# A static planner given a finer picture of its DMA queue, with merged transposes and a mixed load order

One Trainium2 chip, 1 core. The metric is device time of one execution in microseconds, median of several; lower is better.

## What is computed

```python
def _attn_ref(q, k, v, n_sink, window):        # B, H, S, D = 4, 8, 768, 64; 4 sinks, window 128
    scores = (1 / np.sqrt(D)) * np.matmul(q, k.transpose(0, 1, 3, 2))
    keep = is_sink | in_window                 # causal window of 128, and the first 4 keys
    a = softmax(np.where(keep, scores, -1e9))
    return np.matmul(a, v)
def _moe_ref(x, w_in, w_out, beta):            # 3072 tokens, 512 -> 2048 -> 512
    h = x @ w_in
    return (h / (1 + np.exp(-beta * h))) @ w_out
# reference: _moe_ref(attention output as tokens x 512)      [cut]
```

## The kernel before

The work is cut into eight half batches ("hb", 384 tokens) and each into four units (a pair of heads). Python code in the kernel *plans*: a main loop picks the next step for TensorE (T transpose, SC scores, SS sinks, AV values, OT output transpose, H first FFN product, O second), adds its instructions to a graph with estimated durations, and a pass `arrange` then fixes the order on every engine. On the chip nothing is rescheduled: each engine runs its list in order and waits on semaphores. SyncE's list holds every DMA: loads, stores, and DMA transposes (of q and k for half batches 3 to 7, and of the attention output into `xT` for the same; half batches 0 to 2 are transposed on TensorE).

```python
    def place(self, o, at):                      # the planner's clock
        if o.dma:
            self.free[o.eng] = at + o.queue      # queue: 550, or XQ = 1300 for transposes
            self.dma_free = max(self.dma_free, at + 1100) + 1.15 * o.ns
            o.end = self.dma_free + 1000
    ...
    def choose(n):                               # n neighbouring PSUM banks
        runs = [list(range(i, i + n)) for i in range(9 - n) if not held & set(range(i, i + n))]
        return min(((max(G.bank_at(("B", j)) for j in c), c) for c in runs), default=None)
    ...
    def XT(hb, i, c):                            # q: three transposes, k: one
        n, s0 = "qk"[i], 4 * hb % NT
        cs = [c] if i == 0 else list(range(NK))
        ...
    def XO(u):                                   # one transpose for each unit's output
        ...
    LOADS = xl(0) + xl(1) + list(range(16)) + [x for hb in range(2, NSB) for x in xl(hb)]
    OS = [(T_, t, j) for T_ in range(NSB) for t in range(3) for j in range(4)]
    BACKLOG, AHEAD, MARGIN = 6000, 300, 200
```

`list(range(16))` are the sixteen 512 KB weight blocks (eight of w_in, eight of w_out).

The softmax here doesn't subtract the row's maximum and nothing guards it: scores larger than these inputs give would overflow.

Of the kernel before, what the change touches and what calls it, by code (L numbers as in the profile page):

```python
# [21 lines left out]

class Op:
    __slots__ = ("eng", "fn", "deps", "signal", "count", "waits", "sem", "vc", "dma", "seq", "end", "ns", "alts",
                 "group", "tail", "preds", "ready", "left", "succ", "at", "queue")


class Graph:
# [7 lines left out]
    SKIP = 3  # L36
    SLACK = 0
    COLD, WARM = 217, 150

    def __init__(self):  # L40
        self.ops = []
        self.writers = {}
        self.readers = {}
        self.last_x = {}
        self.free = {e: 800.0 for e in self.ENGINES}
        self.dma_free = 0.0
        self.group = 0
        self.filler, self.fill_to = None, 0
# [5 lines left out]
    def add(self, eng, fn, ns=0, r=(), w=(), x=(), dma=None, alts=None, queue=550):  # L54


        o = Op()
        if alts:
            fn, ns = alts[eng]
        o.eng, o.fn, o.dma, o.ns, o.alts = eng, fn, dma, ns, alts or {eng: (fn, ns)}  # L60
        o.queue = queue
        o.signal, o.count, o.waits, o.vc = False, 0, [], None
        o.group = self.group if eng == "pe" else None
        o.seq = len(self.ops)
        deps = []
        for k in r:
            ws = self.writers.get(k)
            assert ws, k
            deps += [(p, True) for p in ws]
        for k in w:  # L70
            deps += [(p, False) for p in self.readers.get(k, ())]
            deps += [(p, False) for p in self.writers.get(k, ())]
        for k in x:
            deps += [(p, False) for p in self.last_x.get(k, ())]
        o.deps = deps
        for k in r:
            self.readers.setdefault(k, []).append(o)
        for k in w:
            self.writers[k] = [o]
            self.readers[k] = []  # L80
        for k in x:
            self.last_x[k] = [o] if eng == "pe" else self.last_x[k] + [o]
        at = self.free[eng]
        for p, _ in deps:
            at = max(at, p.end + (0 if p.eng == eng and not p.dma else self.HOP))
        self.place(o, at)
        self.ops.append(o)
        return o
# [11 lines left out]
    def place(self, o, at):  # L100
        o.at = at
        if o.dma:
            self.free[o.eng] = at + o.queue
            self.dma_free = max(self.dma_free, at + 1100) + 1.15 * o.ns
            o.end = self.dma_free + 1000
        else:
            o.end = self.free[o.eng] = at + o.ns
# [14 lines left out]
    def arrange(self):  # L122
# [22 lines left out]
        self.free = {e: 800.0 for e in self.ENGINES}  # L145
        self.dma_free = 0.0
# [14 lines left out]
        while todo_pe or pool:  # L161
# [14 lines left out]
            for o in pool:  # L176
                opts = []
                for e, (fn, ns) in o.alts.items():
                    t = max(self.free[e], ready(o, e))
                    if o.dma:  # L180
                        t = max(t, self.dma_free - 3000)
                    opts.append((t + ns, t, e))
                _, t, e = min(opts)
                by_eng.setdefault(e, []).append((t, o))
# [161 lines left out]
def _program(nc, G, sb, ps, q, k, v, w_in, w_out, beta, out):  # L346
    NU = 2 * NPAIR
    NSTG, NX, NV, NT, NE, NON, NG, NTT, NOS, NKS, NWS = 2, 2, 3, 8, 4, 4, 3, 3, 3, 4, 6
    XB = 3
    XQ, XNS = 1300, 700  # L350
# [9 lines left out]
    xT = sb("xT", (128, 4, NTOK), BF16)  # L360
# [12 lines left out]
    onorm = sb("onorm", (128, NK, 2, D), BF16, NON)  # L373
# [10 lines left out]
    def add(eng, fn, ns, r=(), w=(), x=(), dma=None, queue=550):  # L384
        return G.add(eng, fn, ns, r, w, x, dma, None, queue)
# [39 lines left out]
    held = {7}  # L425

    def choose(n):

        runs = [list(range(i, i + n)) for i in range(9 - n) if not held & set(range(i, i + n))]
        return min(((max(G.bank_at(("B", j)) for j in c), c) for c in runs), default=None)  # L430
# [66 lines left out]

    def load(hb, n, i):

        b, t0, z = hb // 2, hb % 2 * HALF, hb % NSTG  # L500
        if n == "v":
            src = v[b, :, t0 + i * 128:t0 + (i + 1) * 128, :].rearrange("h p d -> p h d")
            dst, keys, ns = stg[n][z][:, i, :, :], [i], 262144 / 240
        elif hb >= XB:
            src = {"q": q, "k": k}[n][b, :, t0 + i * 128:t0 + (i + 1) * 128, :].rearrange("h p d -> p h d")
            dst, keys, ns = blocks(stg[n][z])[:, i, :, :], [i], 262144 / 240
        else:
            hs = slice(0, H) if i is None else slice(2 * i, 2 * i + 2)
            src = {"q": q, "k": k}[n][b, hs, t0:t0 + HALF, :].rearrange("h (p j) d -> p h (j d)", j=NK)
            dst = stg[n][z][:, hs, :, :].rearrange("p h j d -> p h (j d)")  # L510
            keys, ns = ([i], 196608 / 350) if i is not None else (range(4), 786432 / 350)
        add("sp", lambda e: e.dma_start(dst, src), ns,  # L512
            w=[("stg", n, z, j) for j in keys], dma=f"d{n}{z}{'' if i is None else i}")

    def load_w(j):
# [6 lines left out]
        add("sp", lambda e: e.dma_start(wst[j % NWS], src), 524288 / 370, w=[("wst", j % NWS)], dma=f"dw{j % NWS}")  # L522
# [10 lines left out]
    def cast(hb, n, i):  # L533
# [5 lines left out]
        elif hb == 0:  # L539
# [10 lines left out]
        if hb == 0 and n != "v":  # L550
# [41 lines left out]
    def XT(hb, i, c):  # L592
        n, s0 = "qk"[i], 4 * hb % NT
        cs = [c] if i == 0 else list(range(NK))
# [3 lines left out]
            x16[n][hb % NX][:, cs[0]:cs[0] + len(cs), :, :].rearrange("p c h d -> p (c h d)")), XNS * len(cs),  # L598
            r=[(n + "16", hb % NX, j, c_) for j in range(4) for c_ in cs],
            w=[("qkT", s0 + j, i, c_) for j in range(4) for c_ in cs], dma=f"dx{n}{c}{hb % 2}", queue=XQ)  # L600
# [87 lines left out]
    def AV(u):  # L688
# [5 lines left out]
        for m, ps in enumerate(parts(half)):  # L694
# [20 lines left out]
            onorm[on][:, :, :, :].rearrange("p m h d -> p (m h) d"), av[:, :, 0:D],  # L715
# [4 lines left out]
    def OT(u):  # L720
# [5 lines left out]
        for m in range(NK):  # L726
            add("pe", lambda e, m=m: nc.tensor.transpose(  # L727
                mp[:, m * 128:(m + 1) * 128], onorm[on][:, m, :, :].rearrange("p h d -> p (h d)"), ident[:, :]),
                mm_ns(128), r=[("on", on), "ident"], x=[("B", bs[0])])
        t0 = b * S + half * HALF  # L730
        any_of(copies(xT[:, hp, t0:t0 + HALF], mp[:, 0:HALF], {"dve": 407, "act": 370}),
# [4 lines left out]
    def XO(u):  # L736
        b, half, hp = where(u)
        on = u % NON
        t0 = b * S + half * HALF
        add("sp", lambda e: e.dma_start_transpose(  # L740
            xT[:, hp, t0:t0 + HALF].rearrange("p (m t) -> p m t", t=128),
            onorm[on][:, :, :, :].rearrange("p m h d -> p (m h d)")), XNS * 0.75,
            r=[("on", on)], w=[("xT", hp, 2 * b + half)], dma=f"dy{on}", queue=XQ)
# [3 lines left out]
    def HQ(T_, m):  # L747
# [4 lines left out]
        t0 = T_ * HALF  # L752
        hp = P[:, bs[0], 0:HALF]
        for c in range(4):
            add("pe", lambda e, c=c: e.matmul(  # L755
                hp, w_in16[:, c, m * 128:(m + 1) * 128], xT[:, c, t0:t0 + HALF],
# [9 lines left out]
    o_bank = []  # L766
    os_i = [0]

    def OQ(T_, t, j):
        G.begin()  # L770
        if j == 0:
            o_bank[:] = take(1)
        bk = o_bank[0]
# [5 lines left out]
        if j == 3:  # L779
# [4 lines left out]
            add("sp", lambda e: e.dma_start(out_t[3 * T_ + t], osb[z][:, :]), 262144 / 300, r=[("osb", z)],  # L784
                dma=f"do{z}")
# [5 lines left out]
    def xl(hb):  # L791
        if hb >= XB:
            return [(hb, n, i) for n in "qkv" for i in range(NK)]
        if hb:
            return [(hb, "q", None), (hb, "k", None)] + [(hb, "v", c) for c in range(NK)]
        return [(0, n, i) for i in range(4) for n in "qk"] + [(0, "v", c) for c in range(NK)]

    LOADS = xl(0) + xl(1) + list(range(16)) + [x for hb in range(2, NSB) for x in xl(hb)]
    CASTS = xl(0) + [(hb, n, i) for hb in range(1, NSB) for n in "qkv" for i in range(NK)]
    HS = [(T_, m) for T_ in range(NSB) for m in range(NM)]  # L800
    OS = [(T_, t, j) for T_ in range(NSB) for t in range(3) for j in range(4)]
    n_cast, n_w, n_xt = [0], [0], [4 * XB]
    BACKLOG, AHEAD, MARGIN = 6000, 300, 200

    def head(s):

        i = done[s]
        if s == "T":
            if i >= 4 * XB or i - NT + 4 >= min(done["SC"], done["SS"]):
                return None  # L810
            if n_cast[0] < (2 * i + 2 if i < 4 else 8 + 9 * (i // 4)):
                return None
# [8 lines left out]
        elif s == "AV":  # L821
            if i >= NU or i >= done["OT"] + NON or i >= min(done["SC"], done["SS"]) or n_cast[0] < 11 + 9 * (i // 4):
# [17 lines left out]
        else:  # L840
# [4 lines left out]
            tb = G.bank_at(("B", o_bank[0])) if j else banks_at(1)  # L845
            if j:
                tb = 0
# [11 lines left out]
    def background():  # L859
# [3 lines left out]
        while moved:  # L863
# [17 lines left out]
            if i < len(CASTS):  # L881
                hb, n, c = CASTS[i]
                t = G.at([("in", hb, n, None if n != "v" and 0 < hb < XB else c)])
# [6 lines left out]
            hb, x_ = n_xt[0] // 4, n_xt[0] % 4  # L890
            if XB <= hb < NSB and n_cast[0] > 11 + 9 * (hb - 1) + (x_ if x_ < 3 else 5) and min(done["SC"], done["SS"]) >= 4 * (hb - hb % 2):
                t = G.at([("qk"[x_ // 3] + "16", hb % NX, 0, x_ if x_ < 3 else 2)])
                if t <= now + AHEAD:
                    XT(hb, x_ // 3, x_ % 3)
                    n_xt[0] += 1
                    if n_xt[0] % 4 == 0:
# [5 lines left out]
            if 4 * XB <= done["OT"] < done["AV"]:  # L902
                t = G.at([("onu", done["OT"])])
                if t <= now + AHEAD:
                    XO(done["OT"])
                    done["OT"] += 1
# [8 lines left out]
    for n_, x in enumerate(xl(0)):  # L915
# [4 lines left out]
        if n_ == 5:  # L920
            add("sp", lambda e: e.dma_start(beta_st[:, :], beta.rearrange("(m p) -> m p", p=128)), 20, w=["beta_st"],
                dma="dbeta")
# [37 lines left out]
    while True:  # L960
# [4 lines left out]
        for s in ("OT", "AV", "SC", "SS", "T") + ffn:  # L965
# [3 lines left out]
            if h[0] + (MARGIN if s in ("OT", "AV", "SC", "SS", "T") else 0) <= now:  # L969
                best = (now, s, h[1])  # L970
                break
            if best is None or h[0] + MARGIN < best[0]:
# [48 lines left out]
```

## Time and profile before

| | before |
|---|---|
| time, median of 3 (range) | 236.48 us (236.27 to 237.78) |
| the profiled execution: time, span | 234.82, 232.9 us |
| TensorE paced work / lost / tail | 203.0 / 26.0 / 3.8 us |
| SyncE transposes | 40 |

*Paced work* is the number of matmuls of each kind times their start-to-start distance in a packed stretch; *lost* is the rest up to the last matmul (the prediction shows how both come out).

### The profile page before, as it was taken

What the parts mean: (1) busy time and instruction counts of PE and PEld (TensorE: products, weight loads), DVE (VectorE), ACT (ScalarE), POOL (GpSimd) and SP (SyncE); (2) the same over time, 40 slices, a digit from 0 to 9 for tenths busy, and PEclk for the clock granted to TensorE, in tenths of its full rate; (3) what the DMA queues carried; (4) which work ended last, traced back from release to release, by engine and by line L of the source; (5) the groups of instructions that cost most, each with busy time, mean ns of one, the idle gap of its engine ahead of it and who ended that gap; (6) DMA issues with size and microseconds to landing.
All of it is one profiled execution on the core that took longest, in us unless ns stands there. A gap on an engine that the chain in (4) does not pass through costs nothing.

```text
span 232.9 us, 4577 instructions
## 1 busy us (share of the span) xinstructions
PE 218.9 (94%) x1756; PEld 122.0 (52%) x1756; DVE 136.8 (59%) x291; ACT 152.6 (66%) x276; POOL 72.5 (31%) x163
## 2 busy tenths in 40 slices
PE   7976999899999999998989999999999999999993
PEld 5554555456555555545446555554555555555541
DVE  3795689977764459527739657946553533633310
ACT  3958978578864889439974757776754655645431
POOL 6584943023450337108355104601740000000000
PEclk9999999999999999999999999999999999999999
DMA  6999999999669998694969999977412111011112
GB/s 182 244 335 245 331 363 389 352 235 228 145 155 237 241 272 162 144 176 72 182 133 232 147 227 222 174 170 169 155 34 65 45 45 45 4 45 45 45 48 90
DMA packets 94677, 39.76 MB, mean 171 GB/s; under 512 B 81328, under 2 KB 87488, under 8 KB 94656
## 3 DMA queue, kind: packets, MB, share of 16 engines
q1 hardware_dynamic: 94656, 39.47, 71.4%
q8 instruction: 14, 0.23, 0.4%
q14 instruction: 7, 0.06, 0.1%
HBM read 27.27 MB, written 6.29 MB: 144 GB/s over the span
## 4 chain that ended last, share of the span: by engine, by line
PE 69%; DMA 9%; DVE 8%; ACT 7%; SPq 4%; issue 1%; POOL 0%
PE P L775 34%; PE P L755 26%; DMA v_stage<-in_v_dram 5%; DMA wst<-in_moe_w_in_dram 4%; DVE g L762 3%; ACT E L645 3%; PE P L708 3%; PE P L637 3%; ACT t L760 2%; SPq L740 2%; SPq L512 2%; DVE vaug L453 2%; DVE onorm L714 1%; ACT qkT L448 1%; PE P L698 1%
## 5 line engine op out<-in xcount | busy, mean ns | idle before, releaser
L760 ACT ACTIVATE t<-P,hbeta 128x384 f32<-128x384 f32 x128 | 73.5, 591 | 43.4 <-PE P L755 39.7
L755 PE MATMUL P<-xT,w_in 128*128 128x384 bf16 x512 | 97.3, 326 | 0.9 <-DVE w_in L453 0.6
L775 PE MATMUL P<-w_out,g 128*128 128x512 bf16 x384 | 96.0, 379 | 2.1 <-DVE g L762 1.9
L762 DVE SCALAR_TENSOR_TENSOR g<-t,P 128x384 bf16<-128x384 f32 x128 | 69.2, 548 | 48.4 <-ACT t L760 46.4
L651 POOL TENSOR_SCALAR_AFFINE_SELECT E<-E 128x512 bf16<-128x512 bf16 (+1 forms) x112 | 54.7, 519 | 68.5 <-ACT E L645 67.9
L755 PEld LDWEIGHTS P<-xT,w_in 128*128 128x128 bf16 x512 | 48.0, 98 | 39.3 <-DVE w_in L453 1.4
L775 PEld LDWEIGHTS P<-w_out,g 128*128 128x128 bf16 x384 | 35.9, 98 | 38.3 <-DVE g L762 4.0
L645 ACT ACTIVATE E<-P 128x768 bf16<-128x768 f32 x64 | 45.5, 777 | 5.6 <-PE P L637 5.5
L448 ACT ACTIVATE osb<-P 128x512 f32<-128x512 f32 x19 | 11.4, 598 | 14.6 <-PE P L775 14.6
L708 PE MATMUL P<-vaug,E 128*128 128x65 bf16 x352 | 19.0, 193 | 1.1 <-DVE vaug L453 0.7
L708 PEld LDWEIGHTS P<-vaug,E 128*128 128x128 bf16 x352 | 16.5, 97 | 4.4 <-DVE vaug L453 0.9
L714 DVE TENSOR_TENSOR onorm<-P,rden 128x384 bf16<-128x384 f32 x32 | 17.7, 554 | 0.9 <-DMA xT<-onorm 0.2
L637 PE MATMUL P<-qkT 64*128 64x128 bf16 (+1 forms) x256 | 16.8, 239 | 1.5 <-ACT E L645 1.3
L453 DVE CAST q<-q_stage 128x512 bf16<-128x512 f32 (+1 forms) x19 | 10.1, 541 | 8.5 <-DMA q_stage<-in_q_dram 8.3
L637 PEld LDWEIGHTS P<-qkT 64*128 64x128 bf16 x256 | 8.7, 94 | 11.6 <-issue 4.5
L453 DVE CAST vaug<-v_stage 128x512 bf16<-128x512 f32 x19 | 9.0, 473 | 7.2 <-DMA v_stage<-in_v_dram 7.1
L698 PE MATMUL P<-vS,ES 128*128 128x130 bf16 x64 | 12.7, 220 | 0.0
L712 DVE RECIPROCAL rden<-P 128x6 f32<-128x6 f32 x32 | 6.1, 189 | 9.8 <-PE P L708 9.7
L672 ACT ACTIVATE ES<-P 128x128 bf16<-128x128 f32 (+1 forms) x32 | 11.1, 421 | 0.0
L448 ACT ACTIVATE xT<-P 128x384 bf16<-128x384 bf16 x11 | 5.4, 493 | 7.2 <-PE P L727 7.2
L453 DVE CAST k<-k_stage 128x512 bf16<-128x512 f32 (+1 forms) x15 | 6.9, 465 | 4.9 <-DMA k_stage<-in_k_dram 4.7
L954 PE MATMUL P<-ones 128*128 128x256 bf16 x47 | 8.5, 315 | 1.1 <-POOL ones L459 1.1
(50 smaller groups left out, 101.9 us busy)
## 6 DMA issues: line engine op xcount, KB each, us to landing
v_stage<-in_v_dram SPq DMA_DIRECT2D x24, 256.0 KB, 4.6
out_dram<-osb SPq DMA_DIRECT2D x24, 256.0 KB, 2.4
k_stage<-in_k_dram SPq DMA_DIRECT2D x15, 256.0 KB, 4.6
q_stage<-in_q_dram SPq DMA_DIRECT2D x15, 256.0 KB, 4.8
wst<-in_moe_w_in_dram SPq DMA_DIRECT2D x5, 512.0 KB, 8.6
wst<-in_moe_w_out_dram SPq DMA_DIRECT2D x4, 512.0 KB, 6.8
g<-in_moe_w_out_dram SPq DMA_DIRECT2D x4, 512.0 KB, 7.2
q_stage<-in_q_dram SPq DMA_DIRECT2D x2, 768.0 KB, 7.6
```

Of the source, the lines that this page charges most:

```text
L448: return lambda e: e.activation(dst, src, AF.Copy, bias=0.0, scale=scale)
L453: return lambda e: e.tensor_copy(dst, src)
L637: add("pe", lambda e, dst=dst, own=own, kc=kc, rows=rows, q0=q0, nq=nq: e.matmul(dst, tokens(own, 1, rows, kc, 1)[:, 0, :], tokens(u, 0, r ...
L645: add("act", lambda e, src=src, dst_=dst_: e.activation(dst_, src, AF.Exp, bias=0.0, scale=SCALE), act_ns(256 * n), w=[(k_, z, j) for k_ i ...
L651: add("gp", lambda e, d=d, sg=sg, at_=at_: e.affine_select(d, d, [[0, 2 * len(at_)], [sg, 128]], ALU.is_ge, 0.0, base=min(sg, 0), channel_ ...
L698: add("pe", lambda e, m=m, c0=c0: e.matmul(A[:, c0:c0 + 2 * (D + 1)], ES[z][:, m * 128:(m + 1) * 128], vS[b % 2][:, 2 * hp:2 * hp + 2, :]. ...
L708: e.matmul(A[:, c0:c0 + D + 1], E[z][:, i, hh, :], vaug[vz][:, kb % NK, 2 * hp + hh, :], start=a, stop=o, skip_group_check=True), 39,
L714: add("dve", lambda e: e.tensor_tensor(onorm[on][:, :, :, :].rearrange("p m h d -> p (m h) d"), av[:, :, 0:D], rden[on][:, :].unsqueeze(2) ...
L755: add("pe", lambda e, c=c: e.matmul(hp, w_in16[:, c, m * 128:(m + 1) * 128], xT[:, c, t0:t0 + HALF], start=(c == 0), stop=(c == 3)), mm_ns ...
L760: add("act", lambda e: e.activation(tt[ti][:, :], hp, AF.Tanh, bias=0.0, scale=hbeta[:, m:m + 1]), act_ns(HALF) + 93, r=["hbeta"], w=[("t" ...
L762: add("dve", lambda e: e.scalar_tensor_tensor(gt[T_ % NG][:, m, :], tt[ti][:, :], 1.0, hp, ALU.add, ALU.mult), dve_ns(HALF), r=[("t", ti)] ...
L775: add("pe", lambda e, m=m: e.matmul(P[:, bk, :], gt[T_ % NG][:, m, t * 128:(t + 1) * 128], w_out16[:, m, :], start=(m == 0), stop=(m == NM ...
```

## The change

The intent: give the planner true figures for the SyncE queue, so that it sees when a load or a transpose will really leave; use fewer transposes; bring weights earlier; keep attention groups back until they can run without a stop. The diff, cut to its core (`[cut]` marks cuts; tile layouts changed only so that two units' outputs lie side by side). `RING` is how much the planner lets the queue have under way before it holds the next issue; `FETCH` is transfer time that it sets aside each time TensorE has been given another 256 instructions (a matmul counts as two); a margin (`mg`) is how long the inputs and banks of a step must have been ready before it is taken. One more number changes and is not shown: `SKIP`, how many of TensorE's next groups `arrange` may choose from, goes from 3 to 5.

```diff
+PAR = {'BACKLOG': 3000, 'M_AV': 200, 'M_SC': 1000, 'M_SS': 2000, 'M_T': 500, 'M_OT': 0, [cut]
+ 'mix': 'wawawawwwawawwawwaaawwwawawaaaaa', 'prio': ('SC', 'SS', 'OT', 'AV', 'T')}
+    LEAD = 1500                      # was 3000
+    RING, FETCH = 165, 1100
     def place(self, o, at):
-            self.free[o.eng] = at + o.queue
-            self.dma_free = max(self.dma_free, at + 1100) + 1.15 * o.ns
+            self.pending = [x for x in self.pending if x[0] > at]
+            issued, need = at + o.queue + 40, min(o.ring, self.RING)
+            total = sum(n for _, n in self.pending)
+            for f, n in self.pending:
+                if total + need <= self.RING:
+                    break
+                issued, total = max(issued, f), total - n
+            begin = issued + o.lag if o.lag else at + 1150 + o.ns
+            self.dma_free = max(self.dma_free + o.ns, begin)
+            [cut]
+            if o.eng == "pe":
+                self.n_pe += 2
+                if self.n_pe % 256 == 0:
+                    self.dma_free = max(self.dma_free, at) + self.FETCH
     def choose(n):                   # four banks: two pairs in place of four neighbours
+        if n == 4:
+            pairs = sorted((max(G.bank_at(("B", i)), G.bank_at(("B", i + 1))), i) for i in range(7)
+                           if not held & {i, i + 1})
+            [cut: the two earliest pairs that do not overlap]
-    def XT(hb, i, c):
+    def XT(hb, i):
-        cs = [c] if i == 0 else list(range(NK))
+        cs = list(range(NK))
     def XO(u):
-            xT[:, hp, t0:t0 + HALF].rearrange("p (m t) -> p m t", t=128),
-            onorm[on][:, :, :, :].rearrange("p m h d -> p (m h d)")), XNS * 0.75,
+            xT[:, u // 4, hp:hp + 2, :].rearrange("p h (m t) -> p (h m) t", t=128),
+            onorm[:, on:on + 2, :, :].rearrange("p o m d -> p (o m d)")), 700,
-    LOADS = xl(0) + xl(1) + list(range(16)) + [x for hb in range(2, NSB) for x in xl(hb)]
+    A_, W_ = xl(1) + xl(2), list(range(16))     # hb 1's q, k now in 192 KB pieces
+    LOADS = xl(0)
+    for c_ in PAR['mix']:
+        LOADS.append(A_.pop(0) if c_ == 'a' else W_.pop(0))
+    LOADS += W_ + A_ + [x for hb in range(3, NSB) for x in xl(hb)]
-    OS = [(T_, t, j) for T_ in range(NSB) for t in range(3) for j in range(4)]
+    OS = [(0, t, j) for j in range(4) for t in range(3)]     # hb 0: by weight block
+    OS += [(T_, t, j) for T_ in range(1, NSB) for t in range(3) for j in range(4)]
-            if h[0] + (MARGIN if s in ("OT", "AV", "SC", "SS", "T") else 0) <= now:
+            if h[0] + mg <= now:                 # mg: M_SC and so on, by kind of step
```

## The prediction

> **What bounds the kernel now.** I read the page's engine line first, then the busy time by stretches, then the TensorE and the queue timelines, and last the chain of waits.
>
> ```profile
> PE 218.9 (94%) x1756; PEld 122.0 (52%) x1756; DVE 136.8 (59%) x291; ACT 152.6 (66%) x276; POOL 72.5 (31%) x163
> L755 PE MATMUL P<-xT,w_in 128*128 128x384 bf16 x512 | 97.3, 326 | 0.9 <-DVE w_in L453 0.6
> L775 PE MATMUL P<-w_out,g 128*128 128x512 bf16 x384 | 96.0, 379 | 2.1 <-DVE g L762 1.9
> ...
> 199.41 3.25 PE P L755 x20
> 221.47 7.78 PE P L775 x36
> ```
>
> TensorE is the bound, but its busy time is not its work: durations overlap. The pace of a packed stretch is read from the chain: 3.25 us / 20 = 163 ns for a 384-column matmul, 7.78 / 36 = 216 ns for a 512-column one. In the same way (start to start in the TensorE timeline) the attention matmuls cost 29 ns (65 columns), 57 ns (130), 56 ns (transposes), 51 ns (scores, two row groups side by side), 56 or 163 ns (sinks). Work: 512 x 163 ns = 83.5; 384 x 216 = 82.9; 352 x 29 = 10.2; 64 x 57 = 3.6; 108 x 56 = 6.0; 256 x 51 = 13.1; 16 x 56 + 16 x 163 = 3.5; together **203 us**. The last matmul ends at 229.1 us, so 26.1 us are lost on TensorE, filler matmuls and slow starts included. Span 232.9 = 203 + 26.1 + 3.8 of tail (last copy and store). The measured time, 236.48, is 3.6 above the span.
>
> Where are the 26.1? For each stretch I took its length less the paced work of the matmuls that start in it: 0 to 12 us 8.7; 12 to 23.6 6.7; 23.6 to 30 1.2; 30 to 46 2.0; 46 to 95 1.5; 95 to 130 **4.8**; 130 to 229 1.2. So 18.6 lie before 46 us and 4.8 in one later stretch; the rest is nearly perfect. The stretch view agrees in its weaker measure, TensorE busy:
>
> ```profile
> 12.00:30.00 18.00, 14.02 (x177) 9.24 (x177) 13.03 (x29) 13.98 (x28) 13.50 (x24) 1.00 1.03 305
> 30.00:46.00 16.00, 14.65 (x119) 8.27 (x117) 14.25 (x29) 12.01 (x22) 3.49 (x7) 1.00 1.05 372
> 46.00:95.00 49.00, 48.90 (x410) 27.31 (x409) 33.07 (x73) 38.56 (x72) 18.81 (x41) 1.00 0.98 208
> 95.00:130.00 35.00, 32.24 (x309) 18.10 (x306) 20.79 (x50) 22.80 (x43) 14.50 (x30) 1.00 0.90 161
> 130.00:229.30 99.30, 99.09 (x658) 52.59 (x655) 48.60 (x100) 57.33 (x103) 14.65 (x33) 1.00 0.42 97
> ```
>
> (Columns: stretch, length, busy and count for PE, weight loads, DVE, ACT, POOL, then clock, DMA share, GB/s.) Up to 46 us the DMA engines are full (share 1.03 to 1.05). From 46 to 130 they have room (161 to 208 GB/s against 372 in the weight stretch). So the early loss is arrival of data. The later one I read from the SyncE queue, which issues every load, store and transpose in program order:
>
> ```profile
> 13.39 7.33 SPq L512 DMA_DIRECT2D v_stage<-in_v_dram  x3
> 20.76 0.93 SPq L522 DMA_DIRECT2D wst<-in_moe_w_in_dram  x1
> ...
> 90.03 1.44 SPq L596 DMA_TRANSPOSE qkT<-k  x1
> 91.52 4.21 SPq L596 DMA_TRANSPOSE qkT<-q  x3
> 95.77 2.13 SPq L512 DMA_DIRECT2D q_stage<-in_q_dram  x3
> 98.03 2.77 SPq L596 DMA_TRANSPOSE qkT<-k  x1
> 100.85 4.99 SPq L596 DMA_TRANSPOSE qkT<-q  x3
> 105.88 3.86 SPq L740 DMA_TRANSPOSE xT<-onorm  x3
> 109.79 2.10 SPq L512 DMA_DIRECT2D v_stage<-in_v_dram  x3
> 111.93 6.41 SPq L740 DMA_TRANSPOSE xT<-onorm  x4
> 118.38 2.09 SPq L512 DMA_DIRECT2D k_stage<-in_k_dram  x3
> ```
>
> At 90 to 119 us the queue is solid. The attention output of half batch 3 was computed by about 96 us; three of its four transposes (L740) leave only at 105.88, behind half batch 5's transposes. Meanwhile TensorE spends its spare work, 36 matmuls L775 at 95.3 to 103.1 us, and then has only attention, bound by ScalarE's exponentials: gaps of 0.3 to 0.5 us at 105 to 109. FFN work resumes at 110.4, and attention bunched into it delays tanh: two waits for g, 0.5 us before 115.4 and 1.4 us before 122.7. The chain of waits runs through L740 at 105.88 and the v load at 109.79, so this is on the path.
>
> **What the Trainium skill says.** "TensorE: Matmul & The Clock Gate", Back-to-back issue gap, gives N/2.4 + 2.5 ns warm: 162.5 and 215.8; the trace, 163 and 216, agrees. "DMA: Bandwidth & Descriptors", Why small descriptors are slow, says that HBM transfers in small pieces pay a fixed cost per piece. It agrees: 256 KB loads in 256-byte rows land 1.1 to 1.2 us apart (about 225 GB/s), 512 KB weight loads 1.35 us apart (about 385). "Runtime: NRT & Kernel Launch", Instruction fetch mechanics, says that instructions are fetched by DMA in blocks of 256. The trace has 14 instruction packets of 16 KB on one queue, and 3512 TensorE instructions / 256 = 13.7. "Perfetto Trace Analysis", What "DMA-bound" means, names the issuing sequencer as a limit of its own; the solid queue above is that case.
>
> **The change part by part.** It takes no matmul away: T and OT still serve three half batches, FFN and attention counts stay. 203 us and the 3.8 us tail remain; only lost time can shrink.
>
> *Merged transposes.* Half batches 3 to 7 had 1 k (three blocks), 3 q (one block each) and 4 xT transposes; now 1 k, 1 q and 2 xT: 40 issues become 20. An unheld issue takes 1.26 us for q or xT and 1.44 to 1.53 for the three-block k, so by block count I put a merged q at 1.5 and a paired xT at 1.3. Per half batch: 1.5 + 3 x 1.27 + 4 x 1.27 = 10.4 becomes 3.0 + 2.6 = 5.6. That is 4.8 us of queue time saved each, 24 in all. Most lies beside TensorE's work; only where the queue is solid (90 to 119 us, two half batches, 9.6 us) does it free the path.
>
> *Planner.* The old model puts any load's issue at 550 ns and never holds it. The trace shows 0.47 for row loads, 0.37 for weights, and holds of 1 to 3.5 us when a third 256 KB load follows two others; the new model has 470, 370, a bounded ring, fixed issue times for transposes, and instruction fetches. Loads are planned at most 1.5 us ahead of the transfer queue in place of 3, and the backlog is halved. So the planner should see that L740 would be stuck, and attention groups wait until inputs and banks are 0.5 to 2 us old, letting FFN matmuls fill. With merging I expect 3.5 of the 4.8 us back, not all: ACT must still make 64 exponentials of 777 ns beside 128 tanh of 591 ns. The scattered 1.5 and 1.2 us should give 0.4.
>
> *Load order.* Before: hb1 (2.36 MB), then 16 weight blocks. First weight pair landed 19.5 and 21.0, the second pair 26.6 and 28.2, FFN began at 23.6, weights ended at 45.5. Now weights alternate with 192 KB pieces of hb1. From hb0's last v at 12.1 I add 1.37 us per weight, 0.72 per q/k piece, 1.18 per v: first pair 13.5 and 15.6 (FFN about 17), fourth block 19.8, w_in complete 26.7, first w_out pair 30.2, last v of hb1 42.0, weights complete 43.4. TensorE's possible work by 46 us, at the pace: hb0 attention 4.9, FFN of hb0 10.4 + 10.4, hb1 transposes, scores and sinks 3.7, its AV 2.2, the start of FFN 1 about 0.3: 32 at most, against 46 - 18.6 = 27.4 done before. Ideal loss is then 14 to 15.5. By the same reckoning before could have lost about 14.5 at 29 us and lost 16.5, so I add 2 for casts, hops and copies: 16.2 in place of 18.6, a gain of 2.4. The interleaving starves neither side for long: H0's four quarters need 2.6 us each and arrive 4 to 5 us apart, with hb1 pieces between.
>
> Sum: 2.4 + 3.5 + 0.4 = 6.3 us; 236.5 - 6.3 = **230.2 us**.
>
> **The rivals.** (1) *The early transfer is the bound anyway.* After hb0 the same 10.7 MB must land before both w_out and hb1 are complete, at 44 to 45 us in either order. Now hb1's v comes at 42 in place of 24, so FFN 1 can't start before 45; before, it filled 30 to 45 almost fully (2.0 lost in 16). If the early gain is nil the time is 232.6; if it starves 2 us more, 234.5. For it: DMA share above 1 in both stretches. Against: 6.7 us lost at 12 to 23.6 with no weights in memory. (2) *ScalarE takes the queue's place.* Holding attention back only moves the bunching: ACT was busy 8.7 of 10 us at 110 to 120. Then 95 to 130 keeps 3 of its 4.8 us and the time is about 232. Against: ACT averages 66%, and 130 to 229 us shows attention and FFN together with almost no loss. (3) *Everything fits.* Loss by 46 us falls to 14.5 and later loss to 2: 203 + 16.5 + 3.8 + 3.6 = 226.9 us.
>
> **Range and chances.** The two gains seem independent, each uncertain by 1.5 to 2 us, hence about 2.5 together: 226.8 to 233.5. Two per cent faster is 231.8 us, 1.6 above my value, so faster 0.74; slower needs all gains to vanish and 5 us more, 0.03; the rest 0.23.
>
> **What would show it.** First L755 near 17 us; paced loss before 46 us near 16; 20 transposes on the queue in place of 40 and no half batch's xT transposes more than 4 us after its last onorm; loss in 95 to 130 below 1.5, with waits for g there gone; tail unchanged. A new TensorE gap at 35 to 50 us waiting for v or xT of half batch 1 would be rival 1; waits of L775 for g beside ACT above 85% busy would be rival 2. The prediction is wrong if TensorE's paced work changes, or if the merged transposes are held so long for the ring that they cost the queue what they saved.

## More of the kernel before

One more view, of the xT transposes by their source line (columns: minimum, median, maximum duration in ns on the queue; start of the first and the last):

```profile
L740 SPq DMA_TRANSPOSE xT<-onorm x20: 1180/1257/2391, 85.0 to 174.4; - x20
```

Set beside the DVE instruction that writes the same `onorm`, these leave the queue up to 18.5 us after their input is there (for instance 90.9 us ready, 105.9 us issued).

## The result

| | before | after |
|---|---|---|
| time, median of 4 (range) | 236.98 (236.27 to 237.78) | **230.19** (229.7 to 231.24) |
| ratio, 95% interval | | 0.9718 (0.9667 to 0.9769) |
| profiled execution: time, span | 234.82, 232.9 | 230.38, 228.6 |
| paced work / lost / tail | 203.0 / 26.0 / 3.8 | 203.0 / 22.1 / 3.6 |

Here and below a ratio is the mean time of one kernel's fast runs over the mean of the other's in the same rounds, so it is not quite the ratio of the medians.

The page and the stretches of the changed kernel (columns as in the prediction):

```profile
PE 218.7 (96%) x1756; PEld 121.5 (53%) x1756; DVE 137.1 (60%) x295; ACT 154.0 (67%) x276; POOL 72.6 (32%) x161
```

```profile
12.00:30.00 18.00, 14.98 (x147) 8.78 (x147) 15.81 (x34) 14.24 (x28) 4.60 (x9) 1.00 1.05 367
30.00:46.00 16.00, 15.30 (x153) 8.53 (x149) 11.26 (x21) 11.46 (x20) 10.32 (x16) 1.00 1.01 302
46.00:95.00 49.00, 47.84 (x422) 27.61 (x423) 36.17 (x86) 37.78 (x69) 20.99 (x44) 1.00 1.08 216
95.00:130.00 35.00, 34.52 (x283) 18.25 (x282) 22.93 (x54) 26.25 (x51) 12.43 (x25) 1.00 1.26 216
```

TensorE busy rises at 95 to 130 us from 32.2 to 34.5 of 35, and a little in the two early stretches; at 46 to 95 it falls from 48.9 to 47.8. The same 1756 matmuls run. The queue at the place where it was solid:

```profile
98.53 2.58 SPq L650 DMA_TRANSPOSE qkT<-k  x1
101.15 2.75 SPq L650 DMA_TRANSPOSE qkT<-q  x1
103.94 0.58 SPq L564 DMA_DIRECT2D v_stage<-in_v_dram  x1
104.57 0.58 SPq L834 DMA_DIRECT2D out_dram<-osb  x1
105.19 0.43 SPq L564 DMA_DIRECT2D k_stage<-in_k_dram  x1
105.67 1.48 SPq L791 DMA_TRANSPOSE xT<-onorm  x1
```

Loads and stores now lie between single transposes. No xT transpose leaves more than 1.5 us after its second `onorm` (137.3 ready, 138.8 issued), against 18.5 before. The transposes by line, as above:

```profile
L791 SPq DMA_TRANSPOSE xT<-onorm x10: 1213/1358/1899, 81.6 to 178.4; - x10
```

The durations of all transposes on the queue sum to 59.7 us before (10.0 k, 21.2 q, 28.5 xT) and 35.6 after (8.6, 12.2, 14.7).

### The profile page after: what moved, and what is told of

Same layout as the page of the kernel before. It is cut to its first block, busy times and chain, and to the rows that moved or that the text cites. A ratio compares the mean times of both kernels' runs of the same rounds, so it can differ in the third digit from the quotient of the medians.

```text
span 228.6 us, 4534 instructions
## 1 busy us (share of the span) xinstructions
PE 218.7 (96%) x1756; PEld 121.5 (53%) x1756; DVE 137.1 (60%) x295; ACT 154.0 (67%) x276; POOL 72.6 (32%) x161
## 4 chain that ended last, share of the span: by engine, by line
PE 79%; DVE 7%; DMA 7%; SPq 4%; ACT 2%; issue 1%; POOL 0%; POOLq 0%
PE P L825 33%; PE P L805 30%; PE P L691 5%; DMA q_stage<-in_q_dram 4%; PE P L762 3%; DMA k_stage<-in_k_dram 3%; PE P L1019 2%; SPq L564 2%; PE P L626 2%; DVE onorm L768 2%; DVE g L812 2%; PE P L722 1%; PE P L752 1%; PE P L781 1%; DVE w_in L497 1%; ACT t L810 1%
## 5 line engine op out<-in xcount | busy, mean ns | idle before, releaser
L812 DVE SCALAR_TENSOR_TENSOR g<-t,P 128x384 bf16<-128x384 f32 x128 | 69.0, 550 | 45.2 <-ACT t L810 43.4
L705 POOL TENSOR_SCALAR_AFFINE_SELECT E<-E 128x512 bf16<-128x512 bf16 (+1 forms) x112 | 57.2, 542 | 71.5 <-ACT E L699 71.0
L492 ACT ACTIVATE osb<-P 128x512 f32<-128x512 f32 x22 | 13.1, 597 | 11.5 <-PE P L825 11.3
L762 PE MATMUL P<-vaug,E 128*128 128x65 bf16 x352 | 18.4, 193 | 0.5 <-DVE vaug L497 0.5
L762 PEld LDWEIGHTS P<-vaug,E 128*128 128x128 bf16 x352 | 16.2, 97 | 3.1 <-DVE vaug L497 0.6
L497 DVE CAST q<-q_stage 128x512 bf16<-128x512 f32 (+1 forms) x21 | 10.9, 521 | 8.7 <-DMA q_stage<-in_q_dram 8.7
L691 PE MATMUL P<-qkT 64*128 64x128 bf16 (+1 forms) x256 | 15.8, 239 | 0.1
L711 DVE TENSOR_TENSOR E<-E,maskS 128x512 bf16<-128x512 bf16 x16 | 7.8, 488 | 6.7 <-ACT E L699 6.7
L497 DVE CAST vaug<-v_stage 128x512 bf16<-128x512 f32 x15 | 7.4, 493 | 5.3 <-DMA v_stage<-in_v_dram 5.2
L492 ACT ACTIVATE qkT<-P 128x768 bf16<-128x768 bf16 x10 | 8.1, 820 | 3.7 <-PE P L626 3.7
L497 DVE CAST k<-k_stage 128x512 bf16<-128x512 f32 (+1 forms) x19 | 8.7, 459 | 2.9 <-DMA k_stage<-in_k_dram 2.7
```

Source lines behind the costliest of these rows:

```text
L492: return lambda e: e.activation(dst, src, AF.Copy, bias=0.0, scale=scale)
L497: return lambda e: e.tensor_copy(dst, src)
L691: add("pe", lambda e, dst=dst, own=own, kc=kc, rows=rows, q0=q0, nq=nq: e.matmul(dst, tokens(own, 1, rows, kc, 1)[:, 0, :], tokens(u, 0, r ...
L705: add("gp", lambda e, d=d, sg=sg, at_=at_: e.affine_select(d, d, [[0, 2 * len(at_)], [sg, 128]], ALU.is_ge, 0.0, base=min(sg, 0), channel_ ...
L762: e.matmul(A[:, c0:c0 + D + 1], E[z][:, i, hh, :], vaug[vz][:, kb % NK, 2 * hp + hh, :], start=a, stop=o, skip_group_check=True), 39,
L812: add("dve", lambda e: e.scalar_tensor_tensor(gt[T_ % NG][:, m, :], tt[ti][:, :], 1.0, hp, ALU.add, ALU.mult), dve_ns(HALF), r=[("t", ti)] ...
```

## The experiments

Each edit is to the kernel before ("a") or to the changed one ("u", one part undone). As every order is planned anew from the edit, one edit can move everything behind it; only `e_xo_first` keeps the plan. One table of the losses on TensorE serves all of them (us, paced; four traces lack 25 or 26 records of the O matmul, which come in fours, so the missing ones were filled in: work then sums to 203.0 again). The kernel before ran beside every group of runs, with medians of 235.98 to 237.31 us, so between groups the ratios compare better than the medians; `a_order_pairs`, `a_order_pairs_merge`, `u_pairs` and `u_hold` ran on another chip than the rest. The changed kernel did not run beside the "u" runs, so a cost of undoing a part has no interval of its own.

| run | transposes | 0 to 23.6 | 23.6 to 46 | 46 to 95 | 95 to 130 | 130 to 222 | time | ratio to before (interval) |
|---|---|---|---|---|---|---|---|---|
| before | 40 | 15.4 | 3.2 | 1.5 | 4.8 | 1.0 | | |
| before_again | 40 | 15.6 | 3.4 | 1.3 | 5.2 | 2.0 | 236.56 | (one run) |
| e_xo_first | 40 | 15.4 | 3.4 | 1.4 | 5.7 | 1.4 | 235.97 | 0.9957 (0.9909 to 1.0004) |
| a_merge | 20 | 15.6 | 4.7 | 1.2 | 2.9 | 1.0 | 233.53 | 0.9848 (0.9787 to 0.9908) |
| a_model | 40 | 15.6 | 5.5 | 0.8 | 0.8 | 4.5 | 236.35 | 0.9961 (0.9917 to 1.0005) |
| a_order | 40 | 13.0 | 4.5 | 7.3 | 3.7 | 2.5 | 241.00 | 1.0197 (1.0112 to 1.0283) |
| a_order_pairs | 40 | 13.7 | 3.1 | 2.2 | 3.5 | 5.9 | 237.19 | 1.0023 (0.9973 to 1.0073) |
| a_order_pairs_merge | 20 | 12.9 | 3.5 | 1.8 | 1.9 | 0.9 | **229.36** | 0.9682 (0.9652 to 0.9711) |
| after | 20 | 13.6 | 2.9 | 2.2 | 2.2 | 1.1 | 230.19 | 0.9718 (0.9667 to 0.9769) |
| u_merge | 40 | 13.6 | 2.9 | 1.7 | 6.2 | 1.1 | 234.38 | 0.9911 (0.9842 to 0.9980) |
| u_order | 20 | 15.7 | 3.1 | 1.3 | 3.3 | 1.9 | 234.56 | 0.9935 (0.9836 to 1.0034) |
| u_model | 20 | 13.1 | 4.0 | 5.0 | 1.0 | 0.8 | 232.04 | 0.9809 (0.9726 to 0.9892) |
| u_pairs | 20 | 13.9 | 3.5 | 2.6 | 4.9 | 1.2 | 233.47 | 0.9854 (0.9810 to 0.9897) |
| u_hold | 20 | 13.5 | 3.5 | 2.3 | 2.6 | 2.1 | 233.85 | 0.9874 (0.9831 to 0.9916) |

Four of these profiles hold a stretch of 3.41 us at a granted clock of 0.5, which at half pace costs 1.7 us (an estimate): `e_xo_first` and `u_merge` in 95 to 130, `a_order` and `u_model` in 46 to 95. Their losses there include it.

### The kernel before, profiled again

No edit.

> The kernel before, unchanged, profiled once more. Its profiled execution took 234.8 us, its other runs 236.3 to 237.8, and the profile explains only 4.2 of the 6.8 us between the two kernels. Theory: executions of before differ by 1 to 3 us in how long TensorE waits, so a profile at 236 us or more shows 1 to 3 us more lost time on TensorE, most of it before 46 us or in 95 to 130 us. Rival: the lost time is the same 26 us and the difference lies outside the span.

Time 236.56, span 234.5, lost 27.6: 1.6 us more on TensorE than in the first profile, spread over 95 to 130 and 130 to 222 us (+0.4, +1.0) and the start. Waits for g grew from 1.9 to 3.3 us (first profile, then second):

```profile
PE P L775 <- DVE g L762: 1.9, 2, 1.4
PE P L775 <- DVE g L762: 3.3, 3, 1.7
```

So the size in the theory held, and its rival did not: an ordinary execution of before loses more than the one that had been profiled. The place was missed in part, since 1.0 of the 1.6 us lies after 130. In every profiled run, time less span is 1.7 to 2.1 us; the 3.6 of the prediction had mixed two executions.

### Moving the late transposes only

```diff
+        # after planning: half batch 5's four qkT transposes go behind half batch 3's three late xT transposes
+        keep = [o for o in new if o not in late]
+        at = max(keep.index(o) for o in move) + 1
+        new = keep[:at] + late + keep[at:]
```

> The kernel before with one edit after the planning: on the SyncE queue the four transposes of half batch 5's q and k are put behind the three xT transposes of half batch 3; every other engine's order is untouched. Theory 1 (the queue itself holds TensorE up): loss in 95 to 130 us falls from 4.8 to 3 or less, time 234 to 235. Theory 2 (the lateness acts through the planner, which fixed TensorE's order around it, so that no matmul is waiting for xT): time within 0.7 us of before, loss in that stretch 4 or more.

The queue did as told; the xT transposes left at 98.2 in place of 105.9:

```profile
98.20 4.16 SPq L752 DMA_TRANSPOSE xT<-onorm  x3
102.41 1.51 SPq L608 DMA_TRANSPOSE qkT<-k  x1
103.96 5.00 SPq L608 DMA_TRANSPOSE qkT<-q  x3
```

```profile
PE P L649 <- DMA qkT<-q: 2.0, 1, 2.0
```

There was no gain (ratio 0.9957, 0.9909 to 1.0004). TensorE's order was fixed with attention first, so nobody used the early xT, and the scores now waited 2.0 us for the q that had been moved back: with a crowded queue one wait took the other's place. Theory 1 failed. Theory 2 fits better but is not cleanly shown: the ratio is about 1.0 us, more than its 0.7, though its interval includes that; and of the 5.7 us lost in the stretch about 1.7 is the half clock from 110.8 us, so that without it the loss would be near 4.0 and not above the 4.8 of before.

### The merge alone, and undone

```diff
-        cs = [c] if i == 0 else list(range(NK))
+        cs = list(range(NK))
         # and XO(u) for two units at a time, as in the change
```

> The kernel before with only the transposes merged (one q, one k, two xT per half batch: 20 issues in place of 40), old planner figures, old load order, old margins. Theory of the prediction: the solid queue at 90 to 119 us opens, loss in 95 to 130 falls by 1.5 to 2.5 us, early loss stays 18 to 19, time 234 to 235.5. Rival (the merge alone is hidden, the planner's figures matter): within 1 us of before.

> The changed kernel with only the merging undone (40 transposes again, planned with their own issue times). Theory, after the merge alone gave 1.5% and the planner's figures alone 0.4%: the crowded queue comes back somewhere after 90 us and costs 2 to 3.5 us there; early loss stays 16 to 17; time 232.5 to 234. Rival (with true figures and held attention the planner schedules round 40 transposes): within 1 us of the changed kernel, 229.5 to 231.3.

Alone it gave 1.5% (0.9848), a bit more than expected, with the loss in 95 to 130 down from 4.8 to 2.9. The early stretches got worse by 1.7 us (18 to 19 was expected, 20.3 came), though no merged transpose is issued there: I put that down to replanning. Undone from the changed kernel it cost 4.2 us (234.38 against 230.19), and its place was again 95 to 130 us, where the loss rose from 2.2 to 6.2, more than the 2 to 3.5 expected. True figures and held attention didn't schedule round 40 transposes: xT left up to 19.7 us after its input. Part of the 6.2 is a new cost. The stretches of `u_merge` there (columns as before; the sixth value after the length is the granted clock):

```profile
104.00:108.00 4.00, 2.14 (x38) 1.22 (x35) 1.73 (x5) 4.00 (x10) 4.00 (x10) 1.00 0.54 111
108.00:112.00 4.00, 4.00 (x42) 2.61 (x39) 3.11 (x9) 1.01 (x4) 0.93 (x3) 0.57 0.42 87
```

While only attention was left, ScalarE was busy without a pause and TensorE 2.14 of 4 us; then the granted clock fell to half for 3.41 us. All four executions of `u_merge` show a mean clock of 0.990 or less, about what one such stretch and the low clock at the very end would leave. The same window of 3.41 us at clock 0.5 stands in the middle of `a_order`, `u_model` and `e_xo_first` (TensorE busy 2.60, 2.93 and 1.61 of the 4 us before it), and in neither the first profile of before nor that of the changed kernel. A thin stretch alone does not bring it: in `a_order_pairs` TensorE was busy only 1.39 us from 149 to 153 us and the clock stayed full. "TensorE: Matmul & The Clock Gate", The HAM clock gate, describes a clock that halves after an idle window of about 3.4 us; the length of the half-clock stretch agrees with that window, but TensorE was at no time idle for that long before any of the four.

### The planner's figures alone, and undone

```diff
-            self.free[o.eng] = at + o.queue
-            self.dma_free = max(self.dma_free, at + 1100) + 1.15 * o.ns
+            [the ring, the fetches and the issue times of the change; LEAD 1500; 40 transposes stay]
```

> The kernel before with only the planner's picture of the DMA queue changed (issue times, bounded ring, instruction fetches, lead 1.5 us); the 40 transposes, load order and margins stay. Theory of the prediction: 1 to 2 us off the loss in 95 to 130, early loss 18 to 19, time 234.5 to 236. Rival: nearly all of the late gain comes from here, loss in 95 to 130 about 2.2 as in the changed kernel, time 233.5 to 234.5.

> The changed kernel with only the planner's picture of the DMA queue put back (550 ns per load, 1300 per transpose, no ring, no fetches, lead 3 us). Theory, after the figures alone gave 0.4%: little without crowding, 0.3 to 1.5 us slower than the changed kernel, 230.3 to 232. Rival (the figures are what makes mixing and holding work): 2 us or more slower, 232.2 or more.

Alone: no gain (0.9961). The figures emptied 95 to 130 us (0.8 lost, less than either theory had), but the crowd came back about 48 us later (4.5 lost after 130), and 21.1 us went before 46 where 18 to 19 were expected:

```profile
149.69 4.85 SPq L616 DMA_TRANSPOSE qkT<-q  x3
154.58 3.86 SPq L760 DMA_TRANSPOSE xT<-onorm  x3
```

It is much the picture of 98 to 109 us in the kernel before. Undone, 232.04: slower than the changed kernel by 1.9 us of medians, slightly more than I expected, with 2.8 us lost more at 46 to 95 and 1.2 won back at 95 to 130. This is not clear of noise (the intervals to before, 0.9726 to 0.9892 and 0.9667 to 0.9769, overlap), and about 1.7 of the 2.8 us is the half clock: the two executions with a mean clock of 0.993 took 232.65 and 232.83 us, the two at 0.999 or more 231.09 and 231.44.

### The load order alone, and undone

```diff
-    LOADS = xl(0) + xl(1) + list(range(16)) + [x for hb in range(2, NSB) for x in xl(hb)]
+    [the mixed order, hb 1 in 192 KB pieces, hb 0's second product by weight block, as in the change]
```

> The kernel before with only the load order changed (weights mixed with 192 KB pieces of half batch 1, first FFN's second product by weight block), 40 transposes, old planner figures and margins. Theory of the prediction: paced loss before 46 us falls by about 2 (18.6 to 16.5), later loss stays 7 to 8, time about 2 us below before, 234.5 to 235.5. Rival 1 of the prediction (the same bytes must land, FFN 1 starts later): early gain is given back at 35 to 60 us, loss before 60 us unchanged within 0.7 us, time within 1 us of before.

> The changed kernel with only the load order undone (half batch 1 in 768 KB loads, then all weights). Theory: paced loss before 46 us goes from 16.5 back to 18.5 or so, later loss stays within 1 us, time 2 us above the changed kernel, 231.7 to 233. Rival (load order is hidden, rival 1): within 0.8 us of the changed kernel.

This was the surprise: alone, the order made the kernel about **2% slower** (1.1 to 2.8%). The first 23.6 us gained as meant (15.4 to 13.0), then 7.3 us went between 46 and 95, about 1.7 of it at half clock. TensorE's timeline of `a_order` (start, length, matmuls), and under it that of the changed kernel:

```profile
45.24 3.02 PE L784 MATMUL P<-w_out,g 128*128 128x512 bf16 x12
48.20 1.26 PE L646 MATMUL P<-qkT 64*128 64x256 bf16 x16
...
59.05 1.47 PE L764 MATMUL P<-xT,w_in 128*128 128x384 bf16 x8
```

```profile
36.27 0.50 PE L691 MATMUL P<-qkT 64*128 64x256 bf16 x8
...
40.10 0.51 PE L691 MATMUL P<-qkT 64*128 64x256 bf16 x8
40.54 2.76 PE L825 MATMUL P<-w_out,g 128*128 128x512 bf16 x12
...
48.94 0.81 PE L805 MATMUL P<-xT,w_in 128*128 128x384 bf16 x4
```

In `a_order` the last two score groups of half batch 1 come only when the whole second product is done, at 48.2 us; in the changed kernel they stand between its blocks, at 36.3 and 40.1. So FFN 1 begins at 59.1 in place of 48.9. Undoing the order in the changed kernel cost 4.4 us of medians, twice what I expected: 2.3 more lost before 46 us, 1.9 more in 95 to 222 (5.2 in place of 3.3), 0.9 less at 46 to 95; this profile was 0.5 us quicker than the median. `u_order` puts back the loads alone: half batch 0's second product stays by weight block.

### Load order with the choice of banks

The second product by weight block holds three PSUM banks open at once; my new theory was that a score group that wants four *neighbouring* free banks of eight then finds none.

```diff
-        runs = [list(range(i, i + n)) for i in range(9 - n) if not held & set(range(i, i + n))]
-        return min(((max(G.bank_at(("B", j)) for j in c), c) for c in runs), default=None)
+        [two pairs, as in the change]
```

> The kernel with only the load order changed was 2% slower: the scores of half batch 1's last two units came after the first FFN's whole second product, and FFN 1 began at 59 us instead of 49. New theory: with that product taken by weight block, three PSUM banks stay open, and a score group that asks for four neighbouring banks finds none; the changed kernel takes two pairs. This run is load order plus the pair choice, nothing else: FFN 1 begins at 48 to 51 us, no TensorE loss above 2 us in 46 to 60, time 5 to 7 us below load order alone, 234 to 236. Rival (the old planner figures or the old readiness to take attention first are the reason): FFN 1 still begins after 55 us, time above 238.

> The changed kernel with only the bank choice put back to four neighbours. Theory: score groups of half batch 1 are delayed behind the open product again and FFN 1 begins late, 2 to 5 us slower than the changed kernel, 232 to 235. Rival (held attention and the new figures schedule round it): within 1 us of it.

With nothing but the pairs added, FFN 1 began at 50.4 us, the loss at 46 to 95 fell from 7.3 to 2.2 (about 1.7 of this fall is the half clock, absent here), and the time from 241.0 to 237.2 (ratio to before from 1.0197 to 1.0023). That settles why FFN 1 came late in `a_order`. The time missed the 234 to 236 that I had expected: 5.9 us were lost after 130, where 40 transposes crowd the queue once more and TensorE waits for q:

```profile
145.55 5.34 SPq L613 DMA_TRANSPOSE qkT<-q  x3
150.94 3.85 SPq L757 DMA_TRANSPOSE xT<-onorm  x3
```

```profile
PE P L685 <- DMA qkT<-q: 2.6, 1, 2.6
```

With the pairs undone in the changed kernel, 233.47, as expected in size. But FFN 1 was only 2.2 us later (51.1), and most of the loss lay in 95 to 130 (4.9 in place of 2.2), so here the place was not the one I had named, and why the pairs matter there is not shown.

### Order, pairs and merge, without the new figures and the holding back

```diff
         [a_order_pairs, and the merged XT and XO of a_merge]
```

> The same plus the merged transposes, still with the old planner figures and margins. If the three mechanical parts carry the change: loss before 46 us 16.5 to 17.5, in 95 to 130 2 to 3, time 231 to 232.5, within 1% of the changed kernel. Rival (figures and held attention are needed): 233.5 or more.

**229.36 us**, ratio 0.9682 (0.9652 to 0.9711), at least as good as the whole change (0.9718, 0.9667 to 0.9769; the intervals overlap, so no winner is claimed) and better than the 231 to 232.5 expected. Three mechanical parts carry the gain under the old planner figures and margins, and with the old `SKIP`. The queue where before's had been solid:

```profile
101.39 2.63 SPq L613 DMA_TRANSPOSE qkT<-q  x1
104.06 1.50 SPq L613 DMA_TRANSPOSE qkT<-k  x1
105.61 3.40 SPq L755 DMA_TRANSPOSE xT<-onorm  x2
```

An xT still left up to 5.8 us after its input (127.7 ready, 133.5 issued), so lateness of xT is no measure of the time by itself.

### The holding back undone

```diff
- 'BACKLOG': 3000, 'M_SC': 1000, 'M_SS': 2000, 'M_T': 500, 'M_OT': 0, 'prio': ('SC', 'SS', 'OT', 'AV', 'T')
+ 'BACKLOG': 6000, 'M_SC': 200, 'M_SS': 200, 'M_T': 200, 'M_OT': 200, 'prio': ('OT', 'AV', 'SC', 'SS', 'T')
```

> The changed kernel with only the holding back undone (margins 200 ns for all attention steps, the old priority, backlog 6 us). Theory: holding back only places work that is there anyway; 0 to 1 us slower, 230 to 231.5. Rival (it is what keeps FFN matmuls between attention groups, the prediction's reading): loss in 95 to 130 rises by 1.5 or more, time 232 or more.

233.85: the rival's time, but not at the rival's place, for the loss at 95 to 130 rose by 0.4 only. It is spread: 0.5 before 46, 0.4 there, 1.0 after 130. Its profiled execution (lost 24.3, against 22.1) was again quicker than its median. Yet `a_order_pairs_merge`, with the old margins too, is fast. Set on top of order, pairs and merge, the ratios to before are 0.9682 with neither new figures nor holding back, 0.9874 with the figures alone (`u_hold`), 0.9809 with holding back alone (`u_model`, part of it half clock) and 0.9718 with both (`SKIP` is 3 in the first, 5 in the others): each alone came out slower than neither, and both together no faster. What stays open is why, and how much each is worth in general; a single plan for each setting can't tell, since replanning alone moved stretches by up to 2 us (1.7 in `a_merge` before 46 us).

## Why the prediction came out as it did

The time (230.2 against 230.19) was right, but not for the reasons given: two terms erred and nearly cancelled (the last point), and of the parts that were to bring the late gain the planner's figures were not needed. The range, 226.8 to 233.5, is 3.3 us to either side, wider than the 2.5 us that the text names for it; the text doesn't say why.

- **Early loss.** Predicted 16.2 us by 46 us, measured 16.5; FFN begins at 17.2 (about 17 predicted), the first weight pair lands at 14.2 and 15.9 (13.5 and 15.6), w_in is complete at 27.1 (26.7), half batch 1's last v at 41.2 (42.0), the weights at 45.1 (43.4). The arithmetic of arrivals was right to 1.7 us.
- **But the step missed its condition.** "The interleaving starves neither side for long" looked at arrivals only. `a_order` and `a_order_pairs` show that, under the old planner figures, the order needs the two-pair choice of banks, a part of the diff that the prediction did not name. Rival 1 (FFN 1 starts late) came true in `a_order`, with banks as its cause, not bytes. In the changed kernel FFN 1 begins at 48.9 us in place of 41.6, as rival 1 said it must (not before 45), but the early gain stood and 46 to 95 lost only 0.7 us more.
- **Merged transposes.** Predicted 24 us of queue time saved; measured 59.7 less 35.6, so 24.1. That it agrees so closely is luck: the sum took unheld issues, and on the chip both sides were held. Per half batch it was 11.9 us before (10.4 in the sum) and 7.1 after (5.6). A merged q took 1.80 us or more in the changed kernel (predicted 1.5, and 1.38 at the least in `a_merge`), a paired xT 1.36 in the median (1.3). All xT left within 1.5 us of their input (predicted 4).
- **Later loss.** I expected 3.5 of the 4.8 us at 95 to 130 back and a loss there below 1.5; it was 2.6 back, loss 2.2. The waits for g there shrank from 1.9 us to 0.4 (0.2 before each product) and were not gone. The scattered 0.4 did not come: 46 to 95 lost 0.7 more, and after 130 us nothing was won (1.0 and 1.1). ACT was 8.2 of 10 us busy at 110 to 120: rival 2 played a small part at most.
- **Who did it.** "So the planner should see that L740 would be stuck" was wrong as a cause. The new figures with 40 transposes only moved the crowd (`a_model`), and with 20 transposes the old figures did as well (`a_order_pairs_merge`). The merge opened the queue, in all three settings: 1.5% alone (ratio), 1.8% in the changed kernel (medians 234.38 to 230.19), 3.3% on top of order and pairs (237.19 to 229.36). "So this is on the path" was too quick as well: with the three xT moved ahead (`e_xo_first`) TensorE waited for q instead. And after the 36 spare matmuls at 95.3 us four more L775 follow at 103.7 before only attention is left.
- **The constant.** "The measured time, 236.48, is 3.6 above the span" set a quick execution's span beside slower executions' time; within one execution it is 1.9 (234.82 less 232.9). The profiles differ by 4.2 us of span, about 4.0 of it loss and 0.2 tail, where the sum had 6.3. So the sum took 2.1 us too much off the span and carried a constant 1.8 us too large (the changed kernel has 1.8 in place of 3.6); in the time the two nearly cancel. Against the second profile of before, which is an ordinary execution, the parts are 2.5 (0 to 46), -0.9 (46 to 95), 3.0 (95 to 130) and 0.9 (later), together 5.5 us of the 6.2 between these two runs. So the agreement to 0.1 us is luck; that against an ordinary execution the sizes agree to about 1 us is not.
- **The page cited for the pace.** The formula from "TensorE: Matmul & The Clock Gate" (Back-to-back issue gap) is given there for an isolated matmul; for a sustained stream the same section has about 131 ns at 512 columns. The packed stretch here ran at 216 ns, so it agrees with the first and not with the second.

## What to carry to other kernels

Where one queue issues every transfer in a fixed order, count the queue time of its transfers first: halving the number of transposes did more than telling the planner exactly how long each takes, since with too many of them the crowd only changed its place here. A new load order is worth what the steps between can use: check which buffers (here PSUM banks held open) the reordered work blocks. And take the profile's time and span from the same execution before explaining a difference of 2%.

## What the Trainium skill lacked or had wrong

- "TensorE: Matmul & The Clock Gate" (The HAM clock gate) has the clock halve after an idle window. In `u_merge` TensorE was busy 2.29 of the 4 us before the clock went to 0.5 for 3.41 us, and in `u_model` 2.93 of 4 us; in `a_order_pairs` 1.39 of 4 us at 149 to 153 left the clock at full speed. Which share of activity decides is not on the page, and these runs don't settle it.
- "DMA: Bandwidth & Descriptors" has no measured trn2 figure for how long a DMA transpose of these sizes occupies the issuing queue (its one table of such costs is about trn3, with cycle counts for unnamed earlier chips beside it): here at least 1.18 us for one of three blocks of 128 columns, 1.21 for six, 1.27 for twelve (a k in `a_merge`), so nearly a fixed cost for each issue.
- The same page says nothing of how much an issuing queue can have outstanding before it is held: 256 KB loads in 256-byte rows take 0.47 us to issue, but up to 5.1 us when others are still under way (a v load at 29.5 us of the changed kernel).
- "Runtime: NRT & Kernel Launch" (Instruction fetch mechanics) agreed in number (14 packets of 16 KB) but has no figure for what a fetch costs the data transfers beside it; nor was that measured here apart from the rest of the planner's figures.
